# Linear attention followed by a gated long convolution: keys and queries of four batches turned by crossbar transfers, and a new way of planning the order

## The chip, the cores and the metric

The kernel runs on one core of one Trainium2 chip. A core has five engines that run side by side, each through its own list of instructions: TensorE (PE in the profile, with its weight loads as PEld), VectorE (DVE), ScalarE (ACT), GpSimd (POOL) and SyncE (SP), which only issues transfers here. The metric is the device time of one execution in microseconds (us), as the median of several runs. A profile of one execution has a span of its own, which is a little shorter than the device time.

## The reference

What is computed, cut to what matters. There are 8 batches of 8 heads, 576 rows and 64 columns; the result of the attention is the input of the convolution.

```python
def _attn_ref(q, k, v, omega):                 # q, k, v: 8 x 8 x 576 x 64, omega: 128 x 64
    q_s, k_s = q * scale, k * scale
    def phi(x):
        h = einsum('bhsd,md->bhsm', x, omega) - sum(x * x) / 2
        return exp(h - max(h)) / sqrt(m)
    q_p, k_p = phi(q_s), phi(k_s)
    kv = einsum('bhsm,bhsd->bhmd', k_p, v)
    z = sum(k_p, axis=2)
    return einsum('bhsm,bhmd->bhsd', q_p, kv) / (einsum('bhsm,bhm->bhs', q_p, z) + 1e-6)

def _moe_ref(x, w_proj, filter_fft, w_out):    # x: 8 x 576 x 512
    x1, x2, x3 = split(x @ w_proj, 3)
    x2_conv = irfft(rfft(x2, axis=1) * rfft(filter_fft, axis=0))
    return (x1 * x2_conv * x3) @ w_out
```

## The kernel before

The kernel does not write its instructions in the order in which they are to run. It records them all (`Plan.record`), each with a due date, then works out an order with durations of its own (`Plan.order`, `Plan.simulate`), and issues them in that order; therefore nearly every line of the profile bears one line number, 376. The due date of an instruction is its batch plus figures for its stage, found by a search:

```python
def _new(self, eng, name):
    stage, b = self.where
    due = b + LEAD[stage] + SHIFT.get(self.where, 0.0) + LEAN.get((stage, eng), 0.0)
    op = Op(eng, due, len(self.ops), name, self.where)
...
# in simulate(): of the instructions that can start soon, an engine takes the one due first
soon = min(at for at, _ in cands) + self.WINDOW
at, op = min(
    ((at, op) for at, op in cands if at <= soon), key=lambda c: (c[1].due, c[1].n)
)
```

Consecutive matmuls into one PSUM tile are joined into one planned instruction, so they stay together. The attention of a batch needs keys and queries with the 64 columns of a head on the partitions. They are loaded with rows on the partitions (`kn`, `qn`), turned by TensorE against an identity matrix into a PSUM tile `t` (there is one of it), eight 128x128 blocks at a time, and copied into `kt` and `qt` (one buffer each):

```python
def transposes(dst, srcs, scalar=False):
    ps = bank_t()
    pb = ps[:].bitcast(BF16).rearrange("p (g c) -> p g c", g=8)
    for g, src in enumerate(srcs):
        nc.tensor.transpose(out=pb[:, g, :], in_=src, identity=ident[:])
    if scalar:
        nc.scalar.copy(out=dst, in_=pb[:, 0 : len(srcs)])
    else:
        nc.vector.tensor_copy(out=dst, in_=pb[:, 0 : len(srcs)])
...
kt = nc.tile(att, [P, H, 2, P], BF16, name="kt", bufs=1)
qt = nc.tile(att, [P, NT, NPAIR, P], BF16, name="qt", bufs=1)
# turn_keys(g), g = 0, 1: 8 blocks of kn -> kt, copied by VectorE
# turn_queries(g), g = 0, 1: 8 blocks of qn -> qt, copied by ScalarE from batch 2 on
```

The features of the keys are made a quarter at a time: eight matmuls over 64 partitions, the lower and the upper half of the array in turn, into a tile of two banks (`two_banks`, named `a`; there are two of it), and then one exponential. The queries go the same way, two matmuls of 512 columns for each of four quarters.

```python
rows = [slice(j * D, (j + 1) * D) for j in range(2)]     # D = 64

def key_features(ek_out, kts):
    ps = two_banks()
    for g, kt in enumerate(kts):
        for j in range(2):
            nc.tensor.matmul(out=ps[:, j, g * MF : (g + 1) * MF],
                             lhsT=kt[rows[j]], rhs=om2[rows[j]], start=True, stop=True)
    nc.scalar.activation(out=ek_out, in_=ps[:].rearrange("p j (g m) -> p j g m", m=MF), func=AF.Exp)
...
for g in range(2):
    turn_keys(g)
    for h in (4 * g, 4 * g + 2):
        key_features(ek[:, h : h + 2, :, :].rearrange("p h (u j) m -> p j (h u) m", j=2),
                     [kt[:, hh, u2, :] for hh in (h, h + 1) for u2 in range(2)])
...
for pr in range(NPAIR):                                   # the queries, 4 quarters
    ps = two_banks()
    for j in range(2):
        nc.tensor.matmul(out=ps[:, j, :], lhsT=om2[rows[j]], rhs=qt[rows[j], :, pr, :], ...)
    nc.scalar.activation(out=eqt[:, pr].rearrange("p j t c -> p j (t c)"), in_=ps[:], func=AF.Exp)
```

The last 64 rows of two batches are handled together (`klt`, `qlt`: "left keys", "left queries"), also with matmuls over 64 partitions. Then come the sums over the rows (`sums`), the attention's output turned back (`turn out`), and the convolution: `fold`, `forward`, `gates`, `inverse` and `out`, whose matmuls all use 128 partitions. SyncE issues the small swaps between partition halves (`sw`, `xw`) and the stores; GpSimd issues the loads, which also change the type.

Of the kernel before, what the change touches and what calls it, by code (L numbers as in the profile page):

```python
# [20 lines left out]
P = 128  # L21

LEAD = {
    "filter": -4.02, "fold": 2.53, "forward": 0.13, "gates": 1.25, "inverse": -3.58,
    "keys": -0.74, "left keys": -1.42, "left out": -3.47, "left queries": -2.5,
    "load filter": 4.15, "load k": -3.28, "load kl": -4.87, "load q": -4.83, "load ql": 3.69,
    "load v": -2.57, "load vl": -5.0, "load w0": -1.52, "load w1": 2.2, "load w2": -3.28,
    "out": 0.85, "queries": -3.09, "residues": 3.63, "rest": -0.92, "sines": 0.72, "start": 0.05,
    "sums": -1.73, "tables": 4.64, "turn out": -3.89, "turn queries": -0.32, "values": 4.04,
    "zeros": -3.63,  # L30
}

SHIFT = {
    ("fold", 0): -2.59, ("fold", 1): 1.53, ("forward", 0): 1.64, ("forward", 1): 1.77,
    ("forward", 2): 2.43, ("forward", 6): -1.5, ("gates", 6): 2.79, ("gates", 7): -1.4,
    ("inverse", 1): -1.71, ("keys", 1): 1.17, ("keys", 6): -2.38, ("keys", 7): 1.04,
    ("left keys", 2): 0.82, ("left keys", 6): 1.05, ("load filter", 0): -2.14,
    ("load k", 0): -2.11, ("load k", 1): -1.47, ("load k", 2): -2.04, ("load kl", 0): 2.48,
    ("load q", 0): 0.86, ("load q", 1): 2.2, ("load vl", 0): 2.19, ("load w0", 0): -2.4,
    ("load w1", 0): -0.42, ("load w2", 0): 2.66, ("out", 0): 2.67, ("out", 2): 2.74,  # L40
    ("queries", 2): 1.79, ("queries", 6): 2.39, ("residues", 0): 3.0, ("rest", 7): -2.34,
    ("start", 0): -2.4, ("sums", 1): -2.02, ("turn out", 1): -2.15, ("turn out", 2): -2.12,
    ("turn queries", 2): 1.39, ("turn queries", 6): -1.77, ("turn queries", 7): 2.64,
    ("values", 0): -0.68,
}
LEAN = {
    ("fold", "ACT"): -2.24, ("fold", "DVE"): 2.96, ("fold", "PE"): 2.38, ("forward", "DVE"): 2.74,
    ("forward", "PE"): 1.24, ("gates", "DVE"): -2.41, ("gates", "PE"): 2.89,
    ("inverse", "PE"): 2.53, ("keys", "ACT"): 2.17, ("keys", "DVE"): 1.6, ("keys", "PE"): -0.83,
    ("left keys", "ACT"): 2.87, ("left keys", "PE"): -0.13, ("left queries", "ACT"): 2.39,  # L50
    ("left queries", "PE"): 2.21, ("out", "ACT"): -2.7, ("out", "PE"): 1.93,
    ("queries", "PE"): 2.56, ("residues", "DVE"): -2.83, ("rest", "PE"): -2.83,
    ("sines", "DVE"): -0.9, ("start", "POOL"): -2.18, ("sums", "PE"): -1.08,
    ("tables", "DVE"): 2.34, ("turn out", "ACT"): -2.72, ("turn out", "DVE"): 2.68,
    ("turn out", "PE"): 1.13, ("turn queries", "ACT"): 0.45, ("turn queries", "PE"): -1.72,
# [34 lines left out]
class Op:  # L90
    __slots__ = (
        "eng", "calls", "reads", "writes", "due", "n", "busy", "lat", "deps", "users",
        "tiles", "start", "end", "name", "dma", "table", "where",
    )

    def __init__(self, eng, due, n, name, where):
        self.eng, self.due, self.n, self.name, self.where = eng, due, n, name, where
        self.calls, self.reads, self.writes = [], [], []
        self.busy = self.lat = 0.0
        self.deps, self.users = {}, []  # L100
        self.tiles = set()
        self.dma = self.table = None

# [12 lines left out]
class Plan:  # L116
# [20 lines left out]
    def _new(self, eng, name):  # L137
        stage, b = self.where
        due = b + LEAD[stage] + SHIFT.get(self.where, 0.0) + LEAN.get((stage, eng), 0.0)
        op = Op(eng, due, len(self.ops), name, self.where)  # L140
        self.ops.append(op)
        return op

    def tile(self, pool, shape, dtype, name, bufs=1):
        t = pool.tile(shape, dtype, name=name, bufs=bufs)
        key = t.name if hasattr(t, "name") else t[:].tensor.name
        self.slots[pool.name, name] = bufs
        self.tile_of[key] = ((pool.name, name), self.where[0])
        return t
# [7 lines left out]
    def record(self, eng, real, name, args, kw):  # L157
# [3 lines left out]
        else:  # L161
# [8 lines left out]
            and last.writes[0][0] == outs[0].tensor.name  # L170
        )
        if join:
            op = last
        else:
            op = self._new(eng, f"{name} {outs[0].tensor.name}")
        op.calls.append((real, name, args, kw))
# [22 lines left out]
    def _cost(self, op, eng, name, outs, ins):  # L199
        out = outs[0]  # L200
        n = self._free(out)
        if name == "dma_start":
            a = out if out.space != bass.MemoryType.DRAM else ins[0]
            run = a.ap[-1][1] * SIZE[a.dtype]
            rows = a.ap[0][1] * self._free(a) // a.ap[-1][1]
            if eng == "POOL":
                op.busy, op.lat = (880.0 if rows > 600 else 720.0), 3300.0
                op.dma = ("SW", rows * max(run, 166) / 198.0)
            else:
                op.busy, op.lat = 580.0, 2000.0  # L210
                op.dma = ("HW", rows * run / 180.0 / (1 if out.space == bass.MemoryType.DRAM else 4))
            return
# [32 lines left out]
    def order(self):  # L245
# [23 lines left out]
    def simulate(self):  # L269
# [22 lines left out]
        span, used, slow, table = 0, 0.0, True, "exp"  # L292
        while len(done) < len(ops):
            best = None
            for e in engines:
                cands = []
                for op in ready[e]:
                    at = max(free[e], when[op.n])
                    ok = True
                    for t in op.tiles:  # L300
                        if t in held:
                            continue
                        tag, stage = self.tile_of[t]
                        if head[tag, stage] != place[t] or not slots[tag]:
                            ok = False
                            break
                        at = max(at, min(slots[tag]))
                    if ok:
                        cands.append((at, op))
                if not cands:  # L310
# [3 lines left out]
                    ((at, op) for at, op in cands if at <= soon), key=lambda c: (c[1].due, c[1].n)  # L314
# [23 lines left out]
            free[e] = at + busy  # L338
            if op.dma:
                kind, serve = op.dma  # L340
                go = max(dma_free[kind], at + op.lat)
                if kind == "HW" and dma_free["SW"] > at:
                    go += 2500.0
                dma_free[kind] = go + serve
# [3 lines left out]
            else:  # L348
                op.end = at + lat
            for t in op.tiles:  # L350
# [29 lines left out]
def kernel(  # L380
# [479 lines left out]
    def key_features(ek_out, kts):  # L860

        ps = two_banks()
        for g, kt in enumerate(kts):
            for j in range(2):
                nc.tensor.matmul(
                    out=ps[:, j, g * MF : (g + 1) * MF],
                    lhsT=kt[rows[j]],
                    rhs=om2[rows[j]],
                    start=True,
                    stop=True,  # L870
                )
        nc.scalar.activation(
            out=ek_out, in_=ps[:].rearrange("p j (g m) -> p j g m", m=MF), func=AF.Exp
        )
# [40 lines left out]
    def attention():  # L915
        ekl = None
        for i in range(B // 2):
# [5 lines left out]
            for bb in range(2):  # L923
# [8 lines left out]
                qt = nc.tile(att, [P, NT, NPAIR, P], BF16, name="qt", bufs=1)  # L932

# [38 lines left out]
                def left_keys():  # L972
# [7 lines left out]
                        ekl[:].rearrange("p (g j) m -> p j g m", j=2),  # L980
                        [klt[:, g, :] for g in range(NPAIR)],
# [8 lines left out]
                if b == 0:  # L990
# [4 lines left out]
                    nc.vector.memset(eql[:], 0.0)  # L995
                nc.at("keys", b)
                ek = nc.tile(att, [P, H, NT, MF], BF16, name="ek", bufs=2)
                for g in range(2):

                    turn_keys(g)  # L1000
                    for h in (4 * g, 4 * g + 2):
                        key_features(
                            ek[:, h : h + 2, :, :].rearrange("p h (u j) m -> p j (h u) m", j=2),
                            [kt[:, hh, u2, :] for hh in (h, h + 1) for u2 in range(2)],
                        )
                vc = nc.tile(att, [P, H, NT, D + 2], BF16, name="vc", bufs=2)
# [21 lines left out]
                for g in range(2):  # L1028
                    turn_queries(g)
# [5 lines left out]
                for pr in range(NPAIR):  # L1035
                    ps = two_banks()
                    for j in range(2):
                        nc.tensor.matmul(
                            out=ps[:, j, :],
                            lhsT=om2[rows[j]],  # L1040
                            rhs=qt[rows[j], :, pr, :]
                            if b >= NS
                            else qt[rows[j]].rearrange("p t h c -> p (t h) c")[
                                :, 4 * pr : 4 * pr + 4
                            ],
                            start=True,
                            stop=True,
                        )
                    nc.scalar.activation(
                        out=eqt[:, pr].rearrange("p j t c -> p j (t c)")  # L1050
                        if b >= NS
                        else eqt[:, pr].rearrange("p h (u j) c -> p j (h u) c", j=2),
                        in_=ps[:] if b >= NS else ps[:].rearrange("p j (g c) -> p j g c", c=P),
                        func=AF.Exp,
                    )

# [439 lines left out]
```

## Time and profile before

| | before |
|---|---|
| device time, median of 3 runs | 280.62 us (279.71 to 281.17) |
| span of the profiled execution | 277.8 us |
| PE busy | 257.9 us (93%) |
| DVE busy | 230.5 us (83%) |
| ACT busy | 205.0 us (74%) |
| POOL busy | 62.8 us (23%) |
| packets of the queue of GpSimd's loads, share of 16 engines' span | 60.2% |
| packets of SyncE's queue, share of 16 engines' span | 14.8% |

A group of the profile has the engine, the operation, output and inputs, the shape and the number of instructions; then the busy time in us, the mean duration of one in ns, and how long the engine sat idle just before them and for whom. The ends of matmuls are modelled and overlap: a matmul of 512 columns has a duration of 379 ns but the next one can start much sooner. Therefore what a matmul costs TensorE is read here from start to start, in the list of instructions in order of time: each of its lines has the start in us, the time until the group's last end, the engine, the operation, the operands, the shape and how many were merged.

### The profile page before, as it was taken

To read this page: it belongs to the slowest core of one execution; us is meant where nothing else is said; L and a number is where in the kernel's file an instruction comes from. 1 tells how busy PE (TensorE), PEld (TensorE's weight loads), DVE (VectorE), ACT (ScalarE), POOL (GpSimd) and SP (SyncE) were. 2 spreads that over 40 slices of the span, in tenths; PEclk is the share of its full clock that TensorE was granted. 3 is DMA by queue.
4 is the path that set the end of the run, shared out by engine and by line. 5 is a ranking of instruction groups with operands and counts; after the bars stand their busy time and mean duration, and the time that the engine had idled before them with its cause. 6 is when DMAs were issued, how large, how long until landed. Compare 5 with 4: busy or idle time off the path is not lost. (4 is left out here: it accounts for less than half of the span.)

```text
span 277.8 us, 6079 instructions
## 1 busy us (share of the span) xinstructions
PE 257.9 (93%) x2394; PEld 148.1 (53%) x2394; DVE 230.5 (83%) x500; ACT 205.0 (74%) x311; POOL 62.8 (23%) x86
## 2 busy tenths in 40 slices
PE   1586888999999999999999999999999999999994
PEld 1455765556555567454654755455646545544441
DVE  7879999969579996999998999998696899677650
ACT  1899488687988877999889657968787677654533
POOL 8663664384561161010310100000000000000000
PEclk9995799999999999999999999999999999999999
DMA  7999999999997799022393622333100203441225
GB/s 92 194 186 193 179 182 190 196 138 177 179 164 68 116 133 158 16 18 56 70 127 113 78 76 78 113 114 115 41 1 2 58 2 105 143 151 38 77 76 189
DMA packets 68068, 30.56 MB, mean 110 GB/s; under 512 B 39499, under 2 KB 62536, under 8 KB 68040
## 3 DMA queue, kind: packets, MB, share of 16 engines
q0 software_dynamic: 59616, 17.31, 60.2%
q1 hardware_dynamic: 8280, 12.75, 14.8%
q8 instruction: 18, 0.29, 0.4%
q10 hardware_dynamic: 144, 0.13, 0.1%
q14 instruction: 10, 0.08, 0.1%
HBM read 34.64 MB, written 9.44 MB: 159 GB/s over the span
## 5 line engine op out<-in xcount | busy, mean ns | idle before, releaser
L376 PE MATMUL h<-xt,wproj 128*128 128x512 bf16 x256 | 62.7, 380 | 0.0
L376 ACT CAST x<-h 128x512 bf16<-128x512 f32 x68 | 40.0, 595 | 21.7 <-PE h L376 21.2
L376 PEld LDWEIGHTS <-wproj 128*128 128x128 bf16 x384 | 30.2, 98 | 25.7 <-issue 3.4
L376 ACT ACTIVATE ek<-a 128x1024 bf16<-128x1024 f32 x32 | 32.7, 1049 | 4.7 <-PE a L376 4.7
L376 ACT ACTIVATE osb<-h 128x512 f32<-128x512 f32 (+3 forms) x46 | 26.0, 567 | 11.8 <-PE h L376 8.3
L376 ACT ACTIVATE eqt<-a 128x1024 bf16<-128x1024 f32 x32 | 32.6, 1040 | 1.7 <-PE a L376 1.6
L376 DVE TENSOR_TENSOR x<-h,x 128x512 bf16<-128x512 f32 x32 | 22.0, 688 | 13.0 <-PE h L376 10.0
L376 PE MATMUL h<-wout,yt 128*128 128x512 bf16 x128 | 31.4, 379 | 0.5 <-DVE yt L376 0.3
L376 PE MATMUL h<-wproj,xf 128*128 128x512 bf16 x128 | 31.8, 379 | 0.0
L376 POOL DMA_DIRECT2D qn<-in_q_dram x26 | 23.0, 893 | 25.5 <-PE t L376 18.3
L376 DVE TENSOR_TENSOR xb<-a,rden 128x512 bf16<-128x512 f32 x36 | 24.9, 691 | 1.2
L376 PEld LDWEIGHTS <-yt 128*128 128x128 bf16 x128 | 11.7, 97 | 14.6 <-issue 1.8
L376 DVE TENSOR_TENSOR bt<-h,osb 128x384 f16<-128x384 f32 x32 | 16.3, 550 | 3.3 <-ACT osb L376 2.7
L376 PE MATMUL h<-x,fwb 128*128 128x512 bf16 x72 | 19.0, 379 | 0.0
L376 PEld LDWEIGHTS <-xf 128*128 128x128 bf16 x134 | 12.0, 99 | 11.9 <-issue 0.7
L376 PE MATMUL a<-om,kt 64*128 64x128 bf16 x256 | 14.1, 240 | 3.3 <-DVE kt L376 1.5
L376 PE MATMUL h<-gtab,xs 128*128 128x384 bf16 x64 | 15.6, 326 | 0.0
L376 PEld LDWEIGHTS <-kt 64*128 64x128 bf16 x256 | 8.6, 103 | 11.0 <-issue 7.4
L376 PE MATMUL a<-qt,om 64*128 64x512 bf16 x64 | 12.4, 399 | 2.2 <-ACT eqt L376 1.4
L376 ACT COPY xt<-t 128x1024 bf16<-128x1024 bf16 x12 | 12.2, 1015 | 2.8 <-PE t L376 2.6
L376 ACT COPY qt<-t 128x1024 bf16<-128x1024 bf16 x12 | 12.3, 1024 | 2.5 <-PE t L376 2.5
L376 PE MATMUL t<-ident,xb 128*128 128x128 bf16 x144 | 13.7, 238 | 0.4 <-DVE kt L376 0.2
(167 smaller groups left out, 515.4 us busy)
## 6 DMA issues: line engine op xcount, KB each, us to landing
out_dram<-osb SPq DMA_DIRECT2D x24, 256.0 KB, 2.0
vn<-in_v_dram POOLq DMA_DIRECT2D x8, 512.0 KB, 8.4
kn<-in_k_dram POOLq DMA_DIRECT2D x7, 512.0 KB, 9.0
qn<-in_q_dram POOLq DMA_DIRECT2D x24, 128.0 KB, 5.8
sw<-sp SPq DMA_DIRECT2D x16, 128.0 KB, 2.6
wproj<-in_moe_w_proj_dram POOLq DMA_DIRECT2D x3, 512.0 KB, 9.1
qn<-in_q_dram POOLq DMA_DIRECT2D x2, 512.0 KB, 9.8
out_dram<-xf SPq DMA_DIRECT2D x4, 256.0 KB, 2.0
```

Source lines behind the costliest of these rows:

```text
L376: getattr(real, name)(*args, **kw)
```

## The change

Three things are changed. The keys and queries of batches 4 to 7 are turned by transfers (`dma_start_transpose`), issued by SyncE, one of 128x2048 elements for the keys and one for the queries of a batch; for these batches the transposes on TensorE and the copies out of PSUM are left out. The matmuls over 64 partitions are recorded two tiles at a time (keys and queries), so that planned neighbours stay neighbours. And the planning is different: the due date of an instruction is now computed backwards from its batch's output, along its chain of users, with a figure per stage added; the plan counts 100 ns for each change between matmuls over 64 and over 128 partitions; and it prefers to stay with 64-row matmuls while any can start. All figures of the tables LEAD, SHIFT and LEAN are new, so the whole order of instructions differs.

```diff
+PERIOD, STRETCH, STAY = 110.779, 7.132, 996.75
 LEAD = { ... all figures are new ... }
@@ _cost
+        if name == "dma_start_transpose":
+            op.busy, op.lat = 2000.0, 2200.0
+            op.dma = ("HW", self._free(out) * 128 * 2 / 240.0)
+            return
@@ order
+        for op in reversed(self.ops):
+            lat = op.lat + (op.dma[1] if op.dma else 0.0) + 50.0
+            last = min((u.base for u in op.users), default=op.where[1] * PERIOD)
+            op.base = last - STRETCH * lat / 1000.0
         for op in self.ops:
+            op.due += op.base
@@ simulate
                 at, op = min(
-                    ((at, op) for at, op in cands if at <= soon), key=lambda c: (c[1].due, c[1].n)
+                    ((at, op) for at, op in cands if at <= soon),
+                    key=lambda c: (c[1].due - STAY * (half and c[1].rows == 64), c[1].n),
                 )
...
+                if (op.rows == 64) != half:
+                    half = not half
+                    busy, lat = busy + 100.0, lat + 100.0
...
                 if kind == "HW" and dma_free["SW"] > at:
                     go += 2500.0
+                    if busy > 1000.0:
+                        go, busy = go + 6000.0, busy + 4000.0
@@ key_features
-    def key_features(ek_out, kts):
-        ps = two_banks()
-        ... eight matmuls, one exponential ...
+    def key_features(*units):
+        made = []
+        for ek_out, kts in units:
+            ps = two_banks()
+            made.append(ps)
+            ... eight matmuls ...
+        for ps, (ek_out, _) in zip(made, units):
+            ... one exponential ...
@@ attention
+                crossed = b >= B // 2
+                def cross(dst, src):
+                    nc.sync.dma_start_transpose(out=dst, in_=src)
...
+                if crossed:
+                    nc.at("cross keys", b)
+                    cross(kt[:].rearrange("p h u c -> p (h u) c"),
+                          kn[:].rearrange("p h t d -> p (h t d)"))
+                    nc.at("cross queries", b)
+                    cross(qt[:].rearrange("p t h c -> p (t h) c"),
+                          qn[:].rearrange("p t h d -> p (t h d)"))
                 for g in range(2):
-                    turn_keys(g)
-                    for h in (4 * g, 4 * g + 2):
-                        key_features(...)
+                    if not crossed:
+                        turn_keys(g)
+                    key_features(*((...) for h in (4 * g, 4 * g + 2)))
...
-                    turn_queries(g)
+                    if not crossed:
+                        turn_queries(g)
...
-                for pr in range(NPAIR):
-                    ... two matmuls, one exponential ...
+                for two in ((0, 1), (2, 3)):
+                    ... four matmuls into two tiles, then two exponentials ...
```

More of the change, by code (lines that the diff above doesn't have):

```diff
@@ L21 @@
 P = 128
+PERIOD, STRETCH, STAY = 110.779, 7.132, 996.75
 LEAD = {
[L24 to L28, printed above, removed]
@@ L29 @@
-    "sums": -1.73, "tables": 4.64, "turn out": -3.89, "turn queries": -0.32, "values": 4.04,
-    "zeros": -3.63,
+    "cross keys": -8.69, "cross queries": -12.1, "filter": 3.6, "fold": 1.32, "forward": 26.46,
+    "gates": -2.05, "inverse": 2.98, "keys": -44.78, "left keys": -2.87, "left out": -0.28,
+    "left queries": 0.38, "load filter": -15.08, "load k": 17.16, "load kl": -0.85,
+    "load q": 9.83, "load ql": -0.81, "load v": 8.12, "load vl": 0.04, "load w0": -1.42,
+    "load w1": -2.9, "load w2": 1.71, "out": -19.09, "queries": -0.66, "residues": -3.04,
@@ L31 @@
+    "rest": -35.96, "start": -94.12, "sums": 14.75, "tables": -1.88, "turn out": 0.42,
+    "turn queries": 4.98, "values": 204.41, "zeros": 3.6,
 }
 SHIFT = {
[L34 to L43, printed above, removed]
@@ L44 @@
-    ("values", 0): -0.68,
+    ("forward", 0): -17.5, ("forward", 2): -35.59, ("forward", 7): 31.65, ("gates", 1): -47.99,
+    ("gates", 2): -78.23, ("keys", 6): 46.62, ("keys", 7): 50.83, ("left queries", 1): -15.18,
+    ("load kl", 0): -29.99, ("load ql", 0): 28.1, ("load v", 0): -89.26, ("queries", 6): -56.89,
+    ("rest", 1): 278.3, ("rest", 7): 50.04, ("sums", 2): -15.61, ("sums", 6): -36.73,
+    ("sums", 7): -24.35, ("turn out", 2): -115.3, ("turn out", 6): 1.26, ("values", 0): -174.25,
@@ L45 @@
+    ("values", 2): -204.34,
 }
 LEAN = {
[L47 to L52, printed above, removed]
@@ L53 @@
-    ("sines", "DVE"): -0.9, ("start", "POOL"): -2.18, ("sums", "PE"): -1.08,
-    ("tables", "DVE"): 2.34, ("turn out", "ACT"): -2.72, ("turn out", "DVE"): 2.68,
-    ("turn out", "PE"): 1.13, ("turn queries", "ACT"): 0.45, ("turn queries", "PE"): -1.72,
+    ("fold", "DVE"): -17.73, ("forward", "DVE"): 11.02, ("forward", "PE"): 2.87,
+    ("gates", "PE"): 97.94, ("inverse", "DVE"): 14.74, ("keys", "PE"): -60.85,
+    ("queries", "PE"): -5.83, ("rest", "PE"): -2.62, ("sums", "PE"): -3.28,
+    ("turn out", "DVE"): -5.95, ("turn out", "PE"): -24.15,
@@ L92 @@
         "eng", "calls", "reads", "writes", "due", "n", "busy", "lat", "deps", "users",
-        "tiles", "start", "end", "name", "dma", "table", "where",
+        "tiles", "start", "end", "name", "dma", "table", "where", "rows", "base",
     )
@@ L102, in __init__ @@
         self.dma = self.table = None
+        self.rows = 128
 class Proxy:
@@ L138, in _new @@
         stage, b = self.where
-        due = b + LEAD[stage] + SHIFT.get(self.where, 0.0) + LEAN.get((stage, eng), 0.0)
-        op = Op(eng, due, len(self.ops), name, self.where)
+        more = LEAD.get(stage, 0.0) + SHIFT.get((stage, b), 0.0) + LEAN.get((stage, eng), 0.0)
+        op = Op(eng, more, len(self.ops), name, self.where)
         self.ops.append(op)
@@ L147, in tile @@
         self.slots[pool.name, name] = bufs
-        self.tile_of[key] = ((pool.name, name), self.where[0])
+        line = self.where[0]
+        self.tile_of[key] = ((pool.name, name), "residues" if line == "load filter" else line)
         return t
@@ L169, in record @@
             and last.where == self.where
-            and last.writes[0][0] == outs[0].tensor.name
+            and (
+                last.writes[0][0] == outs[0].tensor.name
+            )
         )
@@ L175, in record @@
             op = self._new(eng, f"{name} {outs[0].tensor.name}")
+            op.rows = ins[0].ap[0][1] if eng == "PE" else 128
         op.calls.append((real, name, args, kw))
@@ L291, in simulate @@
         done, turn = [], {"SW": 0, "HW": 0}
-        span, used, slow, table = 0, 0.0, True, "exp"
+        span, used, slow, half, table = 0, 0.0, True, False, "exp"
         while len(done) < len(ops):
@@ L299, in simulate @@
                     ok = True
[L300 to L304, printed above, removed]
+                    wanted = [t for t in op.tiles if t not in held]
+                    for t in wanted:
+                        key = self.tile_of[t]
+                        ahead = sum(self.tile_of[u] == key and place[u] < place[t] for u in wanted)
+                        more = sum(self.tile_of[u][0] == key[0] for u in wanted)
+                        if head[key] + ahead != place[t] or len(slots[key[0]]) < more:
                             ok = False
                             break
-                        at = max(at, min(slots[tag]))
+                        at = max(at, sorted(slots[key[0]])[more - 1])
                     if ok:
@@ L337, in simulate @@
                 busy, lat = busy + 1283.0, lat + 1283.0
-            free[e] = at + busy
             if op.dma:
@@ L349, in simulate @@
                 op.end = at + lat
+            free[e] = at + busy
             for t in op.tiles:
@@ L858 @@
     rows = [slice(j * D, (j + 1) * D) for j in range(2)]
-    def key_features(ek_out, kts):
-        ps = two_banks()
[L863 to L874, printed above, removed]
+    def key_features(*units):
[3 more added lines that the diff above has]
+            made.append(ps)
+            for g, kt in enumerate(kts):
+                for j in range(2):
+                    nc.tensor.matmul(
+                        out=ps[:, j, g * MF : (g + 1) * MF],
+                        lhsT=kt[rows[j]],
+                        rhs=om2[rows[j]],
+                        start=True,
+                        stop=True,
+                    )
+        for ps, (ek_out, _) in zip(made, units):
+            nc.scalar.activation(
+                out=ek_out, in_=ps[:].rearrange("p j (g m) -> p j g m", m=MF), func=AF.Exp
+            )
     def normalise(ps):
@@ L979, in left_keys @@
                     key_features(
-                        ekl[:].rearrange("p (g j) m -> p j g m", j=2),
-                        [klt[:, g, :] for g in range(NPAIR)],
+                        (
+                            ekl[:].rearrange("p (g j) m -> p j g m", j=2),
+                            [klt[:, g, :] for g in range(NPAIR)],
+                        )
                     )
@@ L995, in attention @@
                     nc.vector.memset(eql[:], 0.0)
+                if crossed:
+                    nc.at("cross keys", b)
+                    cross(
+                        kt[:].rearrange("p h u c -> p (h u) c"),
+                        kn[:].rearrange("p h t d -> p (h t d)"),
+                    )
+                    nc.at("cross queries", b)
+                    cross(
+                        qt[:].rearrange("p t h c -> p (t h) c"),
+                        qn[:].rearrange("p t h d -> p (t h d)"),
+                    )
                 nc.at("keys", b)
@@ L998, in attention @@
                 for g in range(2):
-                    turn_keys(g)
-                    for h in (4 * g, 4 * g + 2):
-                        key_features(
-                            ek[:, h : h + 2, :, :].rearrange("p h (u j) m -> p j (h u) m", j=2),
-                            [kt[:, hh, u2, :] for hh in (h, h + 1) for u2 in range(2)],
+                    if not crossed:
+                        turn_keys(g)
+                    key_features(
+                        *(
+                            (
+                                ek[:, h : h + 2, :, :].rearrange("p h (u j) m -> p j (h u) m", j=2),
+                                [kt[:, hh, u2, :] for hh in (h, h + 1) for u2 in range(2)],
+                            )
+                            for h in (4 * g, 4 * g + 2)
                         )
+                    )
                 vc = nc.tile(att, [P, H, NT, D + 2], BF16, name="vc", bufs=2)
@@ L1034, in attention @@
                 eqt = nc.tile(att, [P, NPAIR, 2, NT, P], BF16, name="eqt", bufs=1)
-                for pr in range(NPAIR):
[L1036 to L1041, printed above, removed]
-                            if b >= NS
[L1043 to L1047, printed above, removed]
-                        )
[L1049 to L1055, printed above, removed]
+                for two in ((0, 1), (2, 3)):
+                    made = []
+                    for pr in two:
+                        ps = two_banks()
+                        made.append((pr, ps))
+                        for j in range(2):
+                            nc.tensor.matmul(
+                                out=ps[:, j, :],
+                                lhsT=om2[rows[j]],
+                                rhs=qt[rows[j], :, pr, :]
+                                if b >= NS
+                                else qt[rows[j]].rearrange("p t h c -> p (t h) c")[
+                                    :, 4 * pr : 4 * pr + 4
+                                ],
+                                start=True,
+                                stop=True,
+                            )
+                    for pr, ps in made:
+                        nc.scalar.activation(
+                            out=eqt[:, pr].rearrange("p j t c -> p j (t c)")
+                            if b >= NS
+                            else eqt[:, pr].rearrange("p h (u j) c -> p j (h u) c", j=2),
+                            in_=ps[:]
+                            if b >= NS
+                            else ps[:].rearrange("p j (g c) -> p j g c", c=P),
+                            func=AF.Exp,
+                        )
```

## The prediction, made before the changed kernel was run

> **What bounds the kernel now.** I read the page's busy slices first, then the busy time by stretch, then TensorE's waits in the steady part, then its instructions in order of time.
>
> The slices (40 of 6.9 us each) show a kernel in two parts:
>
> ```profile
> PE   1586888999999999999999999999999999999994
> DVE  7879999969579996999998999998696899677650
> ACT  1899488687988877999889657968787677654533
> DMA  7999999999997799022393622333100203441225
> ```
>
> For about 45 us TensorE is not full, and the transfers are; from then on PE is at 9 up to the last slice. The stretches say it with numbers (after the length come the busy times of PE, PEld, DVE, ACT and POOL, then granted clock, DMA share and GB/s):
>
> ```profile
> 0.00:45.50 45.50, 30.32 (x368) 22.06 (x369) 40.07 (x100) 33.27 (x40) 28.62 (x43) 0.89 1.54 172
> 45.50:210.00 164.50, 164.15 (x1645) 92.98 (x1643) 144.71 (x305) 132.51 (x201) 34.22 (x44) 1.00 0.74 103
> 210.00:252.00 42.00, 41.69 (x285) 23.21 (x283) 31.67 (x69) 28.98 (x54) 0.00 (x0) 1.00 0.25 76
> ```
>
> Between 45.5 and 210 us PE is busy 164.15 of 164.50 us, VectorE 88%, ScalarE 81%. The waits of PE between 45.5 and 275 us are, in full:
>
> ```profile
> PE h L376 <- DVE yt L376: 0.3, 1, 0.3
> PE h L376 <- DVE bt L376: 0.2, 1, 0.2
> PE a L376 <- DVE vcl L376: 0.2, 1, 0.2
> ```
>
> So 0.7 us of waits in 230 us: TensorE's own list of work sets the end, and a microsecond taken from that list after 45 us is a microsecond off the span, as long as nothing else becomes late. "Busy" hides what fills this list, because matmuls overlap. In order of time, from start to start:
>
> ```profile
> 109.03 0.62 PE L376 MATMUL t<-ident,xb 128*128 128x128 bf16 x8
> 109.48 0.81 PE L376 MATMUL h<-x,fwb 128*128 128x512 bf16 x3
> 110.23 0.40 PE L376 MATMUL a<-om,kt 64*128 64x128 bf16 x8
> 110.56 0.60 PE L376 MATMUL h<-wproj,xf 128*128 128x512 bf16 x2
> ...
> 113.82 0.61 PE L376 MATMUL t<-ident,kn 128*128 128x128 bf16 x8
> 114.26 1.03 PE L376 MATMUL h<-xt,wproj 128*128 128x512 bf16 x4
> ```
>
> The eight key transposes take 114.26 - 113.82 = 0.44 us, 55 ns each. A matmul of 512 columns takes 0.216 us (median over all that follow one another). The three from 109.48 should therefore end their turn at 110.13; the 64-row group starts at 110.23, **0.10 us** later. That group itself is four pairs of 128 columns, 4 x 0.056 = 0.22 us; the next group starts 0.33 us after it, **0.11 us** more. Over the whole trace the same comes out: a 512-column matmul is followed in 0.216 us by one of its own kind, and in 0.312 us by a 64-row one. A change of row count costs about 0.10 us each way.
>
> If I take the columns of every matmul at these rates, TensorE's list is 230.5 us of streaming, 11.2 us for 114 changes (57 stretches of 64-row matmuls), and 28 us of anything else, of which 24 lie before 45 us. The first two are what the change cuts.
>
> [...] No run here shows a crossbar transfer yet. [...] a `sw` swap of 128 KB on SyncE's queue takes 2.6 us at the median, 4.3 us at most.
>
> **Part 1, the transposes.** Batches 4 to 7 have 2 groups of keys and 2 of queries each, 16 groups of 8; 16 x 0.45 us = **7.2 us** less on PE. All of them stand in the full stretch (in the trace, batch 4's keys are turned at 73.8 us, batch 7's last queries at 198.9 us). Beside it go the copies:
>
> ```profile
> L376 DVE COPY kt<-t 128x1024 bf16<-128x1024 bf16 x16 | 10.9, 684 | 3.0 <-PE t L376 2.9
> L376 ACT COPY qt<-t 128x1024 bf16<-128x1024 bf16 x12 | 12.3, 1024 | 2.5 <-PE t L376 2.5
> ```
>
> 8 x 0.684 = 5.5 us off VectorE, 8 x 1.02 = 8.2 us off ScalarE. Neither sets the end, so I count nothing for them; they keep both engines below PE when the span shrinks: DVE 139 us of some 154, 90%, where it was 88%.
>
> **Part 2, fewer changes of row count.** Of the 57 stretches 45 lie after 45.5 us. With two tiles together a batch needs two for keys and two for queries: 6 batches (2 to 7) x 4 = 24, and about 7 for the left keys and queries, 31 in all. So 14 fewer, each with two changes of 0.10 us: 2.8 us. The preference for staying will merge some neighbours, though there are only two `a` tiles and each is held for an exponential of 1.04 us before it is free again; I give it 3 more stretches, 0.6 us. Together **3.4 us**. The 12 stretches before 45.5 us count nothing, since PE waits there anyway.
>
> **Part 3, the new order.** The first 45 us are set by loads at 172 GB/s and by chains of keys, values and sums, with a mean granted clock of 0.80 between 20 and 45.5 us. In them PE streams only some 17 us of work. All loads have new due dates, so this may move by 2 or 3 us either way; that someone searched again, now with the changes of row count in the plan, speaks for a little gain: **-0.5 us**.
>
> **Part 4, new waits.** Eight transfers join SyncE's queue, which issues only swaps and stores: in the trace nothing between 0.7 and 71.5 us, and after that seldom. `kt` and `qt` have one buffer each, so a transfer can't start before the last matmul on the batch before, and must land before the first of its own batch. In the trace the keys of batch 4 are turned from 74 us, of batch 5 from 86, of batch 6 from 114 and of batch 7 from 147, so 12 to 33 us lie between. The plan's own entries in the diff, which are assumptions, come to 2.2 + 2.2 = 4.4 us for a transfer alone and 2.5 + 6.0 us more beside loads, so 4.4 to 12.9 us: it fits if they are near the truth. Since the order is fixed beforehand, each microsecond that a transfer lands later than planned stops PE for as long. I expect most to fit and one or two to be late by a microsecond, or to hold up a swap: **+1.5 us**; and +0.5 us for VectorE at 90%.
>
> **The sum:** -7.2 - 3.4 - 0.5 + 2.0 = -9.1 us, 271.5 us. Where PE was 99% busy with an earlier search, the new one will likely leave few waits as well, and I choose a little lower: **270.0 us**.
>
> **The rivals.** (a) *The transfers become the wait.* [...] with a queue held up by the loads (the DMA row is at 9 until 83 us and at 7 to 9 for two slices more, when batches 4 and 5 are turned), the eight would cost up to 5 us each in PE waits, and `sw` swaps behind them would delay the spectra: 275 to 295 us. For it speaks that no trace shows such a transfer; against it that SyncE's queue is nearly empty and that the row falls to 0 to 3 after 100 us. (b) *VectorE becomes the bound.* It is 90 to 95% busy in several stretches; then the gain of PE would be only part used, some 5 us, 275 us. Against it: its own load falls too. (c) *Everything fits and the start is better as well:* the full 10.6 us plus merged stretches plus 3 us from the start, 264 us.
>
> **Range and chances.** Mechanism and sizes read from a full engine make a gain near certain if the transfers land in time. From rival (c) to a mild form of (a) I take 263.5 to 277.5 us. Faster by over 2% means below 275.0 us: 0.80. Within 2% needs most of the gain to be lost to waits: 0.13. Slower: 0.07, only by (a) in full.
>
> **What would show it.** Right: 128 of the 256 transposes of `kn` and `qn` are left, with 8 `kt` and 8 `qt` copies; the stretches of 64-row matmuls number about 40 instead of 57; PE stays at 9 from about 45 us to the end with waits below 3 us; the crossbar transfers land in 4 to 13 us. Wrong: PE waits on `kt` or `qt` from a DMA by several us, DVE waits on `sw`, or 45 us becomes 50 before PE is full.

## The result, and the profile after

| | before | changed |
|---|---|---|
| device time, median | 280.89 us (279.71 to 281.74) | 269.88 us (268.25 to 270.9) |
| ratio | | 0.9605, 95% interval 0.9541 to 0.967 |
| span of the profiled execution | 277.8 us | 266.5 us |
| PE, DVE, ACT busy | 257.9, 230.5, 205.0 us | 244.2, 222.0, 194.9 us |

The changed kernel is 4.0% faster. Its page's slices (6.7 us each) keep the shape of before, TensorE full from the eighth slice to the end; what is new is that the transfers stay high, with short dips, until 147 us (22 slices), where they fell off after some 110 us before:

```profile
PE   0278688999999999999999999999999999999994
DVE  7879998759987889999989786999999886378780
ACT  1796587676999978799755896999746967756633
DMA  6999999999999997989969342515613123201406
```

The stretches of the changed kernel, with the columns of before, and all waits of PE between 45.5 and 264 us:

```profile
0.00:45.50 45.50, 27.61 (x324) 18.48 (x325) 40.31 (x109) 30.86 (x41) 26.01 (x41) 0.92 1.29 175
45.50:200.00 154.50, 154.13 (x1529) 87.83 (x1527) 134.81 (x279) 123.51 (x192) 36.62 (x45) 1.00 1.11 138
200.00:245.00 45.00, 44.97 (x331) 24.12 (x330) 34.16 (x79) 31.00 (x52) 0.00 (x0) 1.00 0.20 62
```

```profile
PE h L388 <- DVE bt L388: 0.3, 1, 0.3
PE h L388 <- DVE yt L388: 0.3, 1, 0.3
```

TensorE's list still sets the end, with 0.6 us of waits; VectorE is at 87%. Half of the groups that the change takes away are gone (the groups by line, engine and operands):

```profile
L388 PE MATMUL t<-ident,kn 128*128 128x128 bf16 x64 | 6.1, 252 | 4.1 <-DVE klt L388 2.6 <-DVE kt L388 1.5
L388 PE MATMUL t<-ident,qn 128*128 128x128 bf16 x64 | 5.7, 242 | 0.0
L388 DVE COPY kt<-t 128x1024 bf16<-128x1024 bf16 x8 | 5.5, 686 | 0.4 <-PE t L388 0.3
```

In their place stand eight transfers. The views of the tiles `kt` and `qt` give, for SyncE's queue, the ns that one issue took (least, median, most), the first and the last start, and below the us from issue to landing:

```profile
L388 SPq DMA_TRANSPOSE kt<-kn x4: 1598/3006/5849, 67.6 to 166.0; - x4
DMA to landing us min/median/max: 4.3/6.1/14.1
```

```profile
L388 SPq DMA_TRANSPOSE qt<-qn x4: 1333/1392/1989, 91.6 to 186.6; - x4
DMA to landing us min/median/max: 4.5/8.3/12.0
```

The 14.1 us are those of batch 4's keys, begun at 67.6 us beside the loads; the two of batch 7 took 4.3 and 4.5 us. The tightest place is batch 5's keys. In order of time, the last reader of the buffer on PE, the issue on SyncE's queue, and the first reader on PE (three views):

```profile
108.45 0.40 PE L388 MATMUL a<-om,kt 64*128 64x128 bf16 x8
```

```profile
108.88 5.85 SPq L388 DMA_TRANSPOSE kt<-kn  x1
```

```profile
120.11 0.86 PE L388 MATMUL a<-om,kt 64*128 64x128 bf16 x16
```

The buffer is free at 108.8 us, the transfer is issued at once, and 11.2 us later its keys are needed; no wait is seen. The views have the landings of five of the eight transfers, and this is not one of the five; the trace's last packet with its data ended at 116.3 us, 3.8 us before the keys are needed. Here the plan leaves just enough room. The five known ones landed 5.1 to 24.1 us before their first use.

**The account of TensorE.** From the first matmul's start to the last one's, each trace can be split as the prediction did: streaming (columns of all matmuls of the instruction list at the rates given there; the list is taken because some traces lack a few matmul records), changes of row count (at their excess, at most 0.10 us each), and anything else. The experiments below are in the table as well.

| kernel | streaming | changes | else | sum, us |
|---|---|---|---|---|
| before | 230.5 | 11.2 (114) | 28.0 | 269.7 |
| changed | 223.3 | 8.2 (84) | 26.9 | 258.5 |
| 1: changed order, turned on TensorE | 230.5 | 8.2 (84) | 32.2 | 270.9 |
| 2: old order, all crossed | 223.3 | 11.2 (114) | 38.8 | 273.4 |
| 3: stretches split | 223.3 | 12.4 (126) | 28.0 | 263.7 |
| 4: transfers twice | 223.3 | 8.3 (84) | 44.4 | 276.0 |
| 5: transposes without copies | 230.5 | 8.3 (84) | 28.6 | 267.3 |
| 6: old order, batch 4's keys not crossed | 224.2 | 11.2 (114) | 30.8 | 266.2 |
| 7: no preference for staying | 223.3 | 9.8 (100) | 31.5 | 264.7 |
| 8: output of batches 5 to 7 crossed too | 220.7 | 8.5 (86) | 29.9 | 259.0 |

The 11.2 us between the first two rows are 7.2 us of streaming, 3.0 of changes and 1.1 of anything else.

### The profile page after: what moved, and what is told of

Read it like the earlier page. It is cut to its first block, busy times and chain, and to the rows that moved or that the text cites. A ratio compares the mean times of both kernels' runs of the same rounds, so it can differ in the third digit from the quotient of the medians.

```text
span 266.5 us, 5830 instructions
## 1 busy us (share of the span) xinstructions
PE 244.2 (92%) x2266; PEld 138.5 (52%) x2266; DVE 222.0 (83%) x492; ACT 194.9 (73%) x301; POOL 62.6 (24%) x86
## 4 chain that ended last, share of the span: by engine, by line
PE 79%; DVE 13%; ACT 5%; issue 2%; ACTq 0%; DVEq 0%
PE h L388 59%; PE a L388 14%; PE t L388 7%; ACT eqt L388 2%; DVE h L388 1%; DVE bt L388 1%; DVE yt L388 1%; DVE vcl L388 1%; DVE xb L388 1%; DVE xt L388 1%; ACT yt L388 1%; DVE xf L388 1%; DVE x L388 1%; DVE kt L388 1%; ACT ek L388 1%
## 5 line engine op out<-in xcount | busy, mean ns | idle before, releaser
L388 PE MATMUL h<-xt,wproj 128*128 128x512 bf16 x256 | 62.0, 380 | 0.0
L388 PEld LDWEIGHTS <-wproj 128*128 128x128 bf16 x384 | 31.1, 99 | 26.3 <-issue 1.3
L388 ACT ACTIVATE ek<-a 128x1024 bf16<-128x1024 f32 x32 | 32.1, 1040 | 4.0 <-PE a L388 3.9
L388 PE MATMUL h<-wout,yt 128*128 128x512 bf16 x128 | 30.1, 379 | 0.3 <-DVE yt L388 0.3
L388 DVE TENSOR_TENSOR xb<-a,rden 128x512 bf16<-128x512 f32 x36 | 23.3, 675 | 0.3
L388 PEld LDWEIGHTS <-xf 128*128 128x128 bf16 x134 | 12.5, 100 | 12.4 <-PE a L388 0.4
L388 PE MATMUL h<-x,fwb 128*128 128x512 bf16 x72 | 18.3, 379 | 0.0
L388 PEld LDWEIGHTS <-eqt 128*128 128x128 bf16 x256 | 10.8, 98 | 5.4 <-DVE xb L388 1.2
L388 PE MATMUL a<-om,kt 64*128 64x128 bf16 x256 | 12.4, 231 | 1.2 <-DVE kt L388 0.8
L388 PE MATMUL a<-kv,eqt 128*128 128x65 bf16 x256 | 11.9, 194 | 1.2 <-DVE xb L388 0.9
L388 DVE RECIPROCAL rden<-a 128x8 f32<-128x8 f32 x36 | 7.0, 201 | 7.2 <-PE a L388 6.6
```

The source lines that it names most:

```text
L388: getattr(real, name)(*args, **kw)
```

## The experiments

My theory is that TensorE's list of work sets the end, so the transposes and the changes of row count that leave it are the gain, while the transfers are hidden. The rivals are that the gain is the new order's alone, and that the transfers stand at the edge of the path. Two things make plain undoing a poor test here: the planner arranges everything anew after any edit, and its tables were fitted to one plan. Therefore experiments 1 to 6 keep a planned order and change only what is named, in a function `arranged` between planning and issuing. Times are given as ratios to the kernel before in the same series. The changed kernel was run again beside experiments 5 to 7 and beside the last two:

> The changed kernel once more, on the chip of the three runs sent with it, so that they have it beside them: 0.960 of the kernel before, 268 to 270 us.

It came out at 268.9 us, ratio 0.9604 (0.9568 to 0.9641).

> The changed kernel on the chip of the two runs sent with it: 0.960 of the kernel before, 268 to 270 us.

This time 268.3 us, 0.9585 (0.9558 to 0.9612). I use 0.960 below; 0.001 is 0.28 us.

**One edit needed no run.** Recording the matmuls over 64 partitions two tiles at a time does nothing: with that part undone, the instruction lists of all engines are the same, line for line, as the changed kernel's. The planner sorts by due date, and a pair has neighbouring due dates with or without it. Crossing leaves all 114 changes (experiment 2); the new planning without the preference for staying has 100 (experiment 7), with it 84.

**1. The changed order, turned on TensorE.**

```diff
-        for op in self.order():
+        for op in self.arranged(self.order()):
+    # arranged(): each dma_start_transpose gives way to 2 x (8 transposes into t, 1 copy),
+    # the first at the transfer's planned place, where no other t tile is in use
```

> The changed kernel's planned order is kept for everything but the eight transfers: each becomes two groups of eight transposes on TensorE and two copies, placed where the transfer was planned. Theory (TensorE's list sets the end): 16 groups x 0.45 us = 7.2 us more and nothing else, 269.9 + 7.2 = 277 us, up to 279 with waits for the one transpose bank. Rival (the new order, not the transfers, brought the gain; the transposes find gaps): 270 to 272 us.

It took 281.82 us, 1.0064 (1.0043 to 1.0085): 0.0464 or 13 us over the changed kernel. The rival is out; in this order the transfers are worth all of the gain and more. But the theory's 7.2 us are too few. Streaming rises by 7.2 us, and "else" by 5.3. Of PE's waits after 45.5 us the two longest are new:

```profile
PE t L431 <- ACT qt L431: 2.4, 4, 1.2
PE t L431 <- DVE kt L431: 1.2, 2, 0.8
```

TensorE waits for the one transpose bank until a copy has emptied it. These are copies for which the plan had left no place, so some of this may be the insertion's fault; experiment 5 parts the transposes from the copies.

**2. The old order, crossed.**

```diff
+    # arranged(): the 16 groups of transposes of batches 4 to 7 and their 16 copies go;
+    # the transfer goes where its buffer is free and its load has landed by the plan
```

> The kernel before with its own planned order; only the 16 groups of transposes and 16 copies of batches 4 to 7 are taken out and the eight transfers put in, each as soon as its buffer is free and its load has landed. Theory: 7.2 us less, 280.9 - 7.2 = 273.7 us, with 114 changes of row count as before. Rival (transfers become the wait when the order is not made for them): 278 to 285 us, with TensorE waiting on kt or qt from a transfer.

It took 283.67 us, 1.0135 (1.0084 to 1.0186), 3.8 us **slower** than before: the rival's number. The same 7.2 us have left the list, and "else" is 10.8 us larger. On SyncE's queue and on PE, in order of time:

```profile
70.82 4.52 SPq L418 DMA_TRANSPOSE kt<-kn  x1
```

```profile
75.53 1.03 PE L418 MATMUL h<-xt,wproj 128*128 128x512 bf16 x3
83.01 0.61 PE L418 MATMUL a<-om,kt 64*128 64x128 bf16 x8 [6.46 <-DMA kt<-kn]
```

Batch 4's keys were issued at 70.8 us among the loads, took 12.1 us to land, and TensorE stood idle for 6.46 us. The old order has little room at this place. The last matmuls on batch 3's keys and the first on batch 4's, in the kernel before:

```profile
70.38 0.40 PE L376 MATMUL a<-om,kt 64*128 64x128 bf16 x8
76.76 0.40 PE L376 MATMUL a<-om,kt 64*128 64x128 bf16 x8
```

That is 6.0 us from the end of the one to the start of the other. The changed order has 26.7 us there (issue at 67.6 us, first reader below), and so the 14.1 us of its transfer do not show:

```profile
94.31 0.40 PE L388 MATMUL a<-om,kt 64*128 64x128 bf16 x8
```

The wait of experiment 2 is its only long one, but it costs more than itself. The stretches around it (the third column from the right is the granted clock):

```profile
77.00:84.00 7.00, 0.99 (x10) 0.52 (x11) 2.61 (x3) 1.52 (x3) 1.12 (x2) 0.66 2.34 148
84.00:87.50 3.50, 3.50 (x22) 1.15 (x21) 0.00 (x0) 2.16 (x5) 0.14 (x1) 0.70 0.99 152
87.50:91.00 3.50, 3.45 (x51) 2.08 (x48) 2.93 (x7) 2.71 (x5) 2.72 (x4) 1.00 1.14 124
```

The trace's record of the clock has one half from 79.2 to 86.1 us, so work resumes at half speed for some 3 us:

```profile
83.56 1.89 PE L418 MATMUL h<-xt,wproj 128*128 128x512 bf16 x4
85.38 0.61 PE L418 MATMUL a<-qlt,om 64*128 64x512 bf16 x2
```

These four matmuls of 512 columns take 1.82 us from start to start, 0.455 us each against 0.216. The mean granted clock of this trace is 0.974; that of experiment 6, the same order without this one transfer, has 0.987.

**3. Stretches of 64-row matmuls split.**

```diff
+    # arranged(): of two neighbouring 64-row groups, from 45.5 us on, the second is
+    # issued behind the 128-row group that follows; nothing is added or removed
```

> The changed kernel with the same instructions; from 45 us on, 21 stretches of 64-row matmuls are cut in two by moving the second group behind the next 128-row group, which makes 42 more changes of row count. Theory (a change costs TensorE 0.10 us and TensorE sets the end): 42 x 0.098 = +4.1 us, 274 us. Rival (the change of row count is hidden in the pipeline and only looks like a cost): within 1 us of 269.9.

It took 273.03 us, 0.9742 (0.9701 to 0.9782): 0.0142 or 4.0 us over the changed kernel, against 4.1 expected, and the account shows 4.2 us more in changes. With 42 changes more (126 against 84), a change costs 4.0 / 42 = 0.095 us of the end.

**4. Each transfer twice.**

```diff
-            for real, name, args, kw in op.calls:
+            for real, name, args, kw in op.calls * (1 + (op.name[:19] == "dma_start_transpose")):
```

> The changed kernel in the same order, with each crossbar transfer issued twice, one after the other, into the same tile. Theory (the transfers are hidden; from issue to first use there are 9 to 30 us in the trace, to landing 4 to 14): most still fit, keys of batch 5 (11 us) come 2 to 5 us late, and swaps behind them a little: +1 to +6 us, 271 to 276 us. Rival (the transfers already stand at the edge of the path): each of the eight costs its 6 us again, +20 us or more.

It took 284.92 us, 1.0163 (1.0092 to 1.0234): 0.056 or 16 us over the changed kernel. That is far more than the theory allowed. The number is near the rival's, but not for the rival's reason: PE waits for two of the eight pairs alone, the keys and the queries of batch 5. Its three longest waits after 45 us:

```profile
PE a L388 <- DMA qt<-qn: 5.0, 1, 5.0
PE h L388 <- DVE xr L388: 3.9, 1, 3.9
PE a L388 <- DMA kt<-kn: 1.6, 1, 1.6
```

The second of a pair waits for the first and holds SyncE's queue (18.0 us for the first pair of keys), so a swap behind it is issued late (`xw`, which `xr` needs, at 205.04 us, right behind a pair of queries that held the queue from 198.48 to 204.93 us), and the clock halves twice, from 158.4 us for 6.8 and from 209.6 us for 3.4 us (mean granted clock 0.970, against 0.986 in the changed kernel's trace). The three waits are 10.5 us; TensorE works for some 9.3 us at half the clock, which makes another 4.6 (an estimate, half of the 9.3). The edit is rougher than "twice as long". It shows that the transfers are hidden as planned, but that the margin of the tightest is a few us only; I had taken most of 9 to 30 us for margin everywhere.

**5. The transposes without their copies.** The transfers stay and fill `kt` and `qt`; the 128 transposes run too, and their results are dropped.

```diff
-    put += [(j, len(put), transposing), (k, len(put) + 1, copying)]
+    put += [(j, len(put), transposing)]          # and the transfers stay
```

> The changed kernel in its order with its transfers; the 128 transposes of batches 4 to 7 are done on TensorE as well, at the places of the first experiment, but nobody copies their results. Theory (TensorE's list sets the end, and 5 of the 12 us that the first experiment cost came from the copies and the one transpose bank): +7.2 us over the changed kernel, 277 us. Rival (the transposes cost 12 us on TensorE by themselves): 282 us.

It took 277.21 us, 0.9903 (0.9881 to 0.9924): 0.030 or 8.5 us over the changed kernel; 7.2 expected, 12 by the rival. The work of TensorE by itself is the larger part. Experiment 1 has 0.0161 or 4.5 us beyond it. Two things differ between the two: there the copies are done and the transfers are not. As the transfers make PE wait nowhere in the changed kernel, I put the 4.5 us down to the copies, which keep the transpose bank: PE's waits for it are 3.6 us there and 0.6 us here. What the copies cost in time of their own engines isn't shown.

**6. The old order, without the one late transfer.**

```diff
+            if (w, b) == ("k", 4):
+                continue                          # batch 4's keys stay on TensorE
```

> The kernel before in its own order, transfers for batches 4 to 7 but for the keys of batch 4, which stay on TensorE: 14 groups of transposes go. Theory (in the second experiment one transfer, begun beside the loads, cost a wait of 6.5 us and a half clock after it, and the others were hidden): 280 - 14 x 0.45 = 273.7 us, up to 276 with smaller waits. Rival (without an order made for them the transfers make the next one late instead): 280 us or more.

It took 276.36 us, 0.988 (0.9854 to 0.9906), 3.4 us faster than before, where the transfer of batch 4's keys had made it 3.8 us slower. The theory's upper figure fits: of 6.3 us of streaming taken away 2.8 are given back in many small waits (the longest of PE is 0.7 us). So crossing alone, on the old order, brings about a third of the change's gain, and only if the one transfer with 6.0 us of room is left out.

**7. No preference for staying.**

```diff
-PERIOD, STRETCH, STAY = 110.779, 7.132, 996.75
+PERIOD, STRETCH, STAY = 110.779, 7.132, 0.0
```

> The changed kernel with STAY at 0: an instruction over 64 rows is no longer preferred while TensorE is in that mode. The order is planned anew, with the same tables. By the changes of row count alone (100 planned instead of 84): +1.6 us, 271.5 us. Rival (the tables fit one plan, and any other is worse by more than the part that was taken out; the plan's own end is 5.9 us later): 275 us.

It took 274.42 us, 0.9806 (0.9775 to 0.9836): 0.021 or 5.8 us over the changed kernel. The trace has 100 changes, 1.6 us more, and 4.6 us more of anything else, in a plan for which the tables were not made; PE's waits after 45.5 us, 3.6 us where the changed kernel has 0.6, are 3.0 of these. This is the rival's case, and the reason why undoing a part under the planner says little about that part.

**8. Further in the same direction.** Both have new tables.

```diff
+                    elif b in (5, 6, 7):          # and, in the second, (6,)
+                        cross(xt[:, :, t * P : (t + 1) * P], xb[:].rearrange("p c s -> p (c s)"))
                     elif t % 2 == 1:
                         turn_back(...)
```

> The changed kernel carried further: the attention's output of batches 5 to 7 is turned by crossbar transfers as well (four of 128x512 a batch, 12 in all), with tables found by a new search. Theory (TensorE's list sets the end): 48 transposes fewer, 6 groups x 0.45 = 2.7 us, of which the plan keeps 1.8: 267 us, 0.954 of the kernel before. Rival (these transfers stand on the path of their batch, from normalising to folding, and come late): 270 us or more.

> The same for batch 6 alone, four transfers of 128x512: 0.9 us of TensorE's list, of which the plan keeps 0.5: 268.4 us. Rival: a late transfer, 270 us or more.

They took 268.96 us (0.9585, 0.9552 to 0.9619) and 269.1 us (0.9596, 0.957 to 0.9622), beside 0.9585 for the changed kernel: no gain that these runs can show, where the theory had 267 and 268.4 us. The first one's list is 2.6 us shorter, and "else" is 3.0 us longer, in a somewhat slower start and in small waits all along. As the tables are new, the whole order differs, and the runs don't tell whether it or the transfers took back what the list gave. The transfers themselves landed soon, and VectorE waited 1.5 us in all for two of them; the view of `xt` has the issue in ns and the landing in us:

```profile
L632 SPq DMA_TRANSPOSE xt<-xb x12: 1189/1216/2332, 158.7 to 225.6; - x12
DMA to landing us min/median/max: 2.4/2.7/4.4
```

## Why the prediction was right

270.0 us was predicted, 269.88 came out. That the two are 0.12 us apart is luck: its four runs lie between 268.25 and 270.9 us. By the steps:

- **TensorE's list sets the end: right.** Experiments 3 and 5 added 4.2 us of changes and 7.2 us of streaming to the list, and 4.0 and 8.5 us to the time.
- **Part 1, the transposes, -7.2 us: right in size.** Streaming fell by 7.2 us. What I left out is that the copies cost something too, since only one bank serves the transposes: experiment 1 against 5 has 4.5 us for that, with copies put in without a plan.
- **Part 2, fewer changes, -3.4 us: the size was off, and its reason was wrong.** Of 44 stretches after 45.5 us (I had said 45) 33 are left, not 28, so 11 x 0.20 = 2.2 us; with the early ones the account has 3.0. And I credited pairing with most of it, which changes nothing; the planner does it.
- **Part 3, the start, -0.5 us: better than said.** By 60 us TensorE had streamed 28.8 us of work before and 30.0 after, so 1.2 us. This is one execution of each, and the start differs between executions: experiment 4 has the same order there, and its first matmul on batch 2's keys starts at 51.7 us, against 50.2 us in the changed kernel's trace. Of "anything else" a recount of the trace of before finds 22.7 us before 45.5 us, not 24.
- **Part 4, new waits, +2.0 us: they did not come.** PE's waits after 45.5 us went from 0.7 to 0.6 us, and VectorE stood at 87%, not 90. Lowering the sum by 1.5 us, with the reason that the new search would leave few waits, was a guess that came true. The room for the transfers was misread, however. The 12 to 33 us are counted from the turning of one batch to that of the next; from the last matmul on one batch's keys to the first on the next one's, which the prediction itself names as the limit, the order of before has 6.0, 22.3, 4.8 and 35.3 us, and into the first of these the transfer of experiment 2 did not fit. The changed order has 26.7, 11.3, 30.3 and 9.4 us: for batch 4's keys it is the new plan that made the room.
- **Rival (a), the transfers become the wait: false here, true next to it.** Its "up to 5 us each" was my estimate, which no trace had shown. The landings of 4.3 to 14.1 us are close to the range I took from the plan's own entries, 4.4 to 12.9. But the same transfers on the old order make the kernel slower (experiment 2). The chance of it depended on the plan; the profile of before could show that its own order had too little room in places, and not how well the new plan was made. Its DMA row I had misread, too: it stays at 7 to 9 for four slices after 83 us, until 111 us, and is not at 0 to 3 throughout after that.

The parts that failed cancel: 1.2 us less from changes, 0.7 us more from the start, and 2 us of waits that did not come. The total is nearer than its terms, and that is luck as well. What stays open is what the new planning would gain alone, with every batch turned on TensorE and tables searched for that: no run has it, as experiment 1 puts transposes into an order planned without them. Open too is how much of the 4.5 us for copies the old plan paid: there they had places of their own, and no run takes away only them in the order of before.

## What to carry to other kernels

Where one engine is full and hardly waits, read its list from start to start: busy times hid both the 55 ns transposes and the 0.10 us of a change of row count, and both came back as time, nearly one to one. Work that moves from a full engine to a transfer only gains if the fixed order leaves room for the slowest landing, from the last reader of the buffer's old contents to the first of the new: one late transfer of eight turned a gain of 3.4 us into a loss of 3.8. With a planner between the code and the instructions, compare the instruction lists before crediting an edit, and test a part with the order held fixed.

## What the runs showed of the hardware

- A crossbar transfer of 512 KB between SBUF tiles landed in 4.3 and 4.5 us in the changed kernel when the loads were over; the data of the first of these began to move about 1.1 us after its issue and then moved at 184 to 237 GB/s for some 2.3 us. Beside the loads it took 12.0 and 14.1 us there, and 12.1 us in experiment 2, but two others of experiment 2, issued at 91.13 and 100.16 us beside loads, landed in 5.3 and 6.2 us; what makes the difference isn't shown. The longest issue of the changed kernel held SyncE's queue for 5.85 us. One of 128 KB landed in 2.7 us at the median in experiment 8, a plain swap of that size (`sw`) in 2.3 us in the same trace, 2.6 us in the kernel before and 3.7 us in the changed one. From the two sizes, 384 KB more in about 1.7 us (4.4 less 2.7): an estimate of 230 GB/s behind some 2.1 us that do not grow with the size.
- After a wait of 6.46 us on TensorE the clock was at a half for 6.8 us, some 3 us of them with work to do, 0.455 us for a matmul of 512 columns instead of 0.216 (experiment 2): some 1.5 us on top of the wait (an estimate, half of the 3 us). So a late transfer can cost more than its lateness. In experiment 4, with waits of 5.0, 3.9 and 1.6 us, it was at a half twice, for 6.8 and 3.4 us, and not after the shortest. In the kernel before it stood at 0.50 from 22 to 30 us as well, where TensorE is not full; how long a wait it takes isn't shown.
